# The h bias as SyncE's fourth transfer, transposed between dummy matmuls, in a linear-attention and squared-ReLU block

## The chip, the cores and the metric

The kernel runs on one core of a Trainium2 chip. The metric is device time in microseconds (us), the median of several runs. TensorE (PE) does the matmuls and transposes, VectorE (DVE) and ScalarE (ACT) the elementwise work and the evictions from PSUM, GpSimd (POOL) builds constants, and SyncE (SP) issues most DMA transfers.

## The reference

x has 2048 tokens of 448 features in bf16; there are 16 heads of 28. With xn the layer norm of x:

```python
qkv = xn @ wqkv                          # q, k, v by heads
pq, pk = phi(q), phi(k)                  # phi(t) = where(t > 0, t + 1, exp(t)) + 1e-6
kv  = einsum("bhsd,bhse->bhde", pk, v);  z = sum over s of pk
o   = (pq @ kv) / (pq @ z + 1e-6)
s   = o.reshape(...) @ wo
h   = relu(xn @ w1 + b1) ** 2            # 448 -> 1792
g   = silu(h @ w2 + b2)                  # 1792 -> 448
out = x + s * g
```

b1, the h bias, has 1792 numbers. Here it is used as a column of 128 numbers for each of the 14 parts of h.

## The kernel before, in words

The 2048 tokens are 16 tiles of 128. h is 14 parts of 128 features. The 448 input features are three chunks of 128 and a rest of 64; the rests of two token tiles, or of two parts, are multiplied side by side on the two halves of TensorE's rows.

Every operation is recorded with what it reads and writes. TensorE's and SyncE's operations keep the order in which they are recorded; those of the other engines are placed by a planner in the kernel, from assumed durations, due times and (for the first DMA transfers) a written table `landing` of arrival times. The planner also gives PSUM banks to TensorE's results. Semaphore waits are derived from the resulting order. For the first tiles the orders of VectorE and ScalarE are written out as chains (`bn0 ag0 ...`, `rs1 eT0.0 ...`), in which the bias copy `b1f` is the last on ScalarE's chain.

The head of the program, where the change lies:

- SyncE issues x of tile 0, tile 1, tiles 2 and 3; the main k weights (`load_main` with `w_k`, three chunks); the main weights of h parts 0 and 1 and their two rests; b1 as 14 rows of 128 (`b1r`, 256 bytes a row); then the weights of h parts 2 to 5, x of tiles 4 and 5, the weights of parts 6 to 9, x of tiles 6 and 7, the weights of parts 10 to 13, and the later loads. All go through the helper at L429. ScalarE issues the two k-weight rests itself.
- TensorE starts with dummy matmuls (`warm`, L1223), whose results nobody reads. `pe_transpose` (L604) transposes the three chunks of a normalized tile, `pe_transpose_rests` (L628) the rests of two tiles. `k_part` (L803) and `k_rests` (L818) make k of tiles 0 and 1, `head_part(lo, fi)` (L831) makes h part `fi` for tiles `lo` and `lo + 1` from the three main chunks, and `head_rest` (L847) adds the rests of parts 0 and 1 for all four tiles.
- `bias_cols` (L1238, L1241) transposes `b1r` on TensorE, a matmul of 14 rows by 14 columns, and ScalarE copies the result to `b1f`. ScalarE's and VectorE's bias-and-ReLU evictions of h (L766, L763) read `b1f`.
- Evictions of transposed tiles are at L613 and L614 (chunks) and L637 (rests).

After `head_rest` come, on TensorE, the other h parts of the first four tiles (L788), then k, q, the gate (L1094), sums over tokens and the attention product, in a written order. VectorE's transposes serve the later tiles.

The TensorE order of the head in the kernel before, by its own calls:

```python
        pe_transpose(0, ((0, 3, "act"),))
        warm(5)
        pe_transpose(1, ((0, 3, "act"),))
        ...
        head_part(0, 0)
        head_part(0, 1)
        pe_transpose_rests(2, "dve")
        head_part(2, 0)
        head_part(2, 1)
        bias_cols()
        head_rest(0)
```

Of the kernel before, what the change touches and what calls it, by code (L numbers as in the profile page):

```python
# [9 lines left out]
P = 128  # L10
S, D, F = 2048, 448, 1792
# [35 lines left out]
class Program:  # L47
# [6 lines left out]
    def add(self, eng, emit, reads=(), writes=(), dur=0.2, alts=(), nbytes=0, mode=None, label="", slow=1.0):  # L54
        op = Op(eng, emit, reads, writes, dur, alts, nbytes, mode, label)
        op.slow, op.behind, op.at = slow, None, None
        for t in op.reads:
            op.raw.add(self.writer[t])
            self.readers.setdefault(t, []).append(op)
        for t in op.writes:  # L60
            w = self.writer.get(t)
            if w is not None and w is not op:
                op.deps.add(w)
            for r in self.readers.get(t, ()):
                if r is not op:
                    op.deps.add(r)
            self.writer[t] = op
            self.readers[t] = [r for r in self.readers.get(t, ()) if r is op]
        op.raw.discard(op)
        op.deps |= op.raw  # L70
        for d in op.deps:
            d.succ.append(op)
        self.ops.append(op)
        return op
# [233 lines left out]
def bass_recurrent_scan__linear_attn_block__dense_activation_squared_relu__prompt_kernel(  # L308
    nc, A_x, A_wqkv, A_wo, B_x, B_w1, B_b1, B_w2, B_b2, out
):  # L310
    with ExitStack() as es:
# [24 lines left out]
        b1r = sb("b1r", [NF, P], bf)  # L336
# [83 lines left out]
        def tiles(t, lo, hi):  # L420
            if hi <= 2:
                return t[0][P * lo : P * hi].rearrange("(p s) d -> p s d", s=1)
            base, n = (2, 2) if hi <= 4 else (lo // 4 * 4, 4)
            v = t[0][P * base : P * (base + n)].rearrange("(p s) d -> p s d", s=n)
            return v[:, lo - base : hi - base, :]

        def dma(eng, dst, src, writes, nbytes, reads=(), dur=0.45, slow=1.0):
            return add(
                eng, lambda e, _: e.dma_start(dst, src), reads, writes, dur, nbytes=nbytes, label="dma" + str(writes[0]), slow=slow  # L429
            )  # L430

        def load_x(lo, hi, eng="sp"):
            dma(eng, x_tok[:, lo:hi, :], tiles(A_x, lo, hi), [("x", i) for i in range(lo, hi)], (hi - lo) * P * D * 2)

        def load_main(eng, w, src, name, lo, hi, c0=0, c1=3, off=0):
            dma(
                eng, w[:, c0:c1, lo:hi],
                src[128 * c0 : 128 * c1, off + lo : off + hi].rearrange("(c p) j -> p c j", p=P),
                [(name, c) for c in range(c0, c1)], 128 * (c1 - c0) * (hi - lo) * 2,
            )  # L440

        def load_rest(eng, w, src, name, lo, hi, off=0, part=None):
            for i in (0, 1) if part is None else (part,):
                dma(
                    eng, w[64 * i : 64 * i + 64, 3, lo:hi], src[384:448, off + lo : off + hi], [(name, 3 + i)],
                    64 * (hi - lo) * 2, ["actw"] if eng == "act" else (), dur=0.58,
                )
# [5 lines left out]
        load_x(0, 1, "sp")  # L453
        load_x(1, 2, "sp")
        load_x(2, 4, "sp")
        load_main("sp", w_k, A_wqkv, "wk", 0, D, off=D)
        load_rest("act", w_k, A_wqkv, "wk", 0, D, off=D, part=0)
        load_rest("act", w_k, A_wqkv, "wk", 0, D, off=D, part=1)
        load_main("sp", w_1, B_w1, "w10", cuts[0], cuts[1])
        load_rest("sp", w_1, B_w1, "w10", cuts[0], cuts[1], part=0)  # L460
        load_rest("sp", w_1, B_w1, "w10", cuts[0], cuts[1], part=1)
        dma("sp", b1r[:, :], B_b1.rearrange("(f p) -> f p", p=P), ["b1r"], F * 2)
        for i in (1, 2, 3):
            name = f"w1{i}"
            if i == 2:
# [130 lines left out]
        def pe_transpose(si, pieces):  # L596
            for lo, hi, eng in pieces:
                b = Buf("T")

                def f(e, _, lo=lo, hi=hi, b=b):  # L600
                    v = ps(b)[:, :].bitcast(bf)
                    last = None
                    for c in range(lo, hi):
                        last = e.transpose(v[:, (c - lo) * P : (c - lo + 1) * P], xn[:, si, c * P : (c + 1) * P], ident[:, :])  # L604
                    return last

                add("pe", f, [("xn", si), "ident"], [b], (0.107 if si < 2 else 0.0558) * (hi - lo), mode="128", label=f"T{si}.{lo}")

                def ev(e, eng, lo=lo, hi=hi, b=b):
                    src = ps(b)[:, 0 : 64 * (hi - lo)].bitcast(bf)  # L610
                    dst = xT[:, si, lo:hi, :].rearrange("p c k -> p (c k)")
                    if eng == "dve":
                        return e.tensor_copy(dst, src)  # L613
                    return e.activation(out=dst, in_=src, func=AF.Copy)  # L614

                n = hi - lo
                add(
                    eng, ev, [b], [("xT", si, c) for c in range(lo, hi)],
                    0.15 + 0.07 * n if eng == "dve" else 0.18 + 0.107 * n, label=f"eT{si}.{lo}",
                ).prio = -30  # L620

        def pe_transpose_rests(lo, eng):
            b = Buf("T")

            def f(e, _):
                v = ps(b)[:, :].bitcast(bf)
                for i in range(2):
                    last = e.transpose(v[:, i * P : (i + 1) * P], xn[:, lo + i, 384:512], ident[:, :])  # L628
                return last

            ts = (lo, lo + 1)
            add("pe", f, [("xd", i) for i in ts] + ["ident"], [b], 0.0558 * 2, mode="128", label=f"TR{lo}")

            def ev(e, eng):
                src = ps(b)[:, 0:P].bitcast(bf).rearrange("p (t k) -> p t k", t=2)
                if eng == "dve":
                    return e.tensor_copy(xT[:, lo : lo + 2, 3, :], src)  # L637
                return e.activation(out=xT[:, lo : lo + 2, 3, :], in_=src, func=AF.Copy)

            add(eng, ev, [b], [("xT", i) for i in ts], 0.39 if eng == "act" else 0.25, label=f"eTR{lo}").prio = -30  # L640
# [187 lines left out]
        def head_part(lo, fi):  # L828
            def f(e, _):
                for c in range(3):  # L830
                    last = e.matmul(  # L831
                        ps(head[fi])[:, lo * P : (lo + 2) * P], w_1[:, c, fi * P : (fi + 1) * P], xT[:, lo : lo + 2, c, :],
                        start=(lo == 0 and c == 0), stop=False, skip_group_check=True,
                    )
                return last

            add(
                "pe", f, [("w10", c) for c in range(3)] + [("xT", lo + i, c) for i in (0, 1) for c in range(3)] + ([head[fi]] if lo else []),
                [head[fi]], 3 * MM(256), mode="128", label=f"Ha{fi}.{lo}",
            )  # L840
# [376 lines left out]
        def warm(n, after=(), src=None):  # L1217
            b = Buf("W")

            def f(e, _):  # L1220
                last = None
                for _i in range(n):
                    last = e.matmul(ps(b)[:, 0:P], src or dum[:, 0:P], src or dum[:, 0:P], start=True, stop=True)  # L1223
                return last

            add("pe", f, ["dum", *after] if src is None else [], [b], n * 0.107, mode="128", label="warm")
# [8 lines left out]
        def bias_cols():  # L1235
            bb = Buf("B1")
            add(
                "pe", lambda e, _: e.transpose(ps(bb)[:, 0 : NF // 2].bitcast(bf), b1r[:, :], ident[0:NF, 0:NF]),  # L1238
                ["b1r", "ident"], [bb], 0.1, mode="128", label="B1",
            )  # L1240
            add("act", lambda e, _: e.activation(out=b1f[:, :], in_=ps(bb)[:, 0 : NF // 2].bitcast(bf), func=AF.Copy), [bb], ["b1f"], 0.2, label="b1f")  # L1241
# [2 lines left out]
        warm(30)  # L1244
        warm(4, [("mv", 0)])
        pe_transpose(0, ((0, 3, "act"),))
        warm(5)
        pe_transpose(1, ((0, 3, "act"),))
        warm(2)
        pe_transpose_rests(0, "dve")  # L1250
# [3 lines left out]
        k_rests(0)  # L1254
        pe_transpose(3, ((0, 3, "dve"),))
        head_part(0, 0)
        head_part(0, 1)
        pe_transpose_rests(2, "dve")
        head_part(2, 0)
        head_part(2, 1)  # L1260
        bias_cols()
        head_rest(0)

        byname = {op.label: op for op in pr.ops}
        for first, order in (
# [7 lines left out]
            if first < -26:  # L1273
                byname[names[0]].prio = first
        landing = {
# [3 lines left out]
        }  # L1279
        for (name, k), t in landing.items():  # L1280
# [136 lines left out]
```

## Time and profile before

| | |
|---|---|
| median of 3 runs | 143.07 us (143.07 to 143.12) |
| the profiled execution's own time | 142.37 us |
| its span, first to last instruction | 141.1 us |
| granted TensorE clock in the span | 1.00 |
| TensorE busy | 137.6 us, 1299 matmuls |
| VectorE, ScalarE, GpSimd busy | 104.0, 77.4, 6.3 us |
| DMA | 12.91 MB, mean 91 GB/s over the span |

Times in the profile are microseconds from the start of the span. A timeline line gives the start, the time from the first to the last of a group, the engine, the source line, the operation, the tiles and shapes, and in brackets the idle time before it with what ended it. PEld is TensorE's weight load, which runs beside its matmuls; the recorded end of a matmul includes the time to drain, so matmuls that follow each other overlap in the listing. SPq and ACTq are the issues of DMA transfers by those engines. A transfer has landed when the last of its completion marks is there; those times are read from the trace.

### The profile page before, as it was taken

What the parts mean: (1) busy time and instruction counts of PE and PEld (TensorE: products, weight loads), DVE (VectorE), ACT (ScalarE), POOL (GpSimd) and SP (SyncE); (2) the same over time, 40 slices, a digit from 0 to 9 for tenths busy, and PEclk for the clock granted to TensorE, in tenths of its full rate; (3) what the DMA queues carried; (4) which work ended last, traced back from release to release, by engine and by line L of the source; (5) the groups of instructions that cost most, each with busy time, mean ns of one, the idle gap of its engine ahead of it and who ended that gap; (6) DMA issues with size and microseconds to landing.
All of it is one profiled execution on the core that took longest, in us unless ns stands there. A gap on an engine that the chain in (4) does not pass through costs nothing.

```text
span 141.1 us, 3239 instructions
## 1 busy us (share of the span) xinstructions
PE 137.6 (97%) x1299; PEld 70.9 (50%) x1299; DVE 104.0 (74%) x226; ACT 77.4 (55%) x142; POOL 6.3 (4%) x40
## 2 busy tenths in 40 slices
PE   7999999999999999999999999999999999999992
PEld 7764445454444544444444444435447455555472
DVE  1988992999798898878867799695036516874875
ACT  3759993141988526986952867696138630301312
POOL 7900000000000000000000000000000000000000
PEclk9999999999999999999999999999999999999999
DMA  4999997249923000323000000000796001223033
GB/s 98 277 289 293 312 327 147 40 61 299 178 41 52 5 0 6 50 42 47 12 5 0 0 0 5 0 0 19 183 211 133 0 0 35 96 69 102 33 98 98
DMA packets 24220, 12.91 MB, mean 91 GB/s; under 512 B 14354, under 2 KB 23566, under 8 KB 24206
## 3 DMA queue, kind: packets, MB, share of 16 engines
q1 hardware_dynamic: 22414, 11.35, 31.9%
q10 hardware_dynamic: 1792, 1.36, 4.3%
q8 instruction: 10, 0.16, 0.5%
q14 instruction: 4, 0.03, 0.1%
HBM read 9.23 MB, written 1.90 MB: 79 GB/s over the span
## 4 chain that ended last, share of the span: by engine, by line
PE 93%; DVE 3%; DMA 1%; issue 0%
PE pb L788 29%; PE pb L1094 23%; PE pb L1186 8%; PE pb L889 7%; PE pb L731 7%; PE pb L741 6%; PE pb L1111 4%; PE pb L1151 3%; DMA x_tok<-in_A_x_dram 1%; PE pb L868 1%; DVE st L497 1%; DVE gbuf L1175 1%; PE pb L895 1%; PE pb L831 1%; PE pb L1038 1%; PE pb L803 1%
## 5 line engine op out<-in xcount | busy, mean ns | idle before, releaser
L788 PE MATMUL pb<-xT,w 64*128 64x512 bf16 x378 | 43.6, 376 | 0.0
L1094 PE MATMUL pb<-w,r 64*128 64x448 bf16 x336 | 34.6, 349 | 0.0
L766 ACT ACTIVATE r<-pb,b1f 128x512 bf16<-128x512 f32 x39 | 25.2, 686 | 12.3 <-PE pb L788 12.0
L788 PEld LDWEIGHTS pb<-xT,w 64*128 64x128 bf16 x378 | 18.4, 94 | 21.7 <-DMA w<-in_B_w_dram 0.2
L1094 PEld LDWEIGHTS pb<-w,r 64*128 64x128 bf16 x336 | 16.3, 94 | 15.9 <-issue 0.4
L778 ACT ACTIVATE r<-r 128x1024 bf16<-128x1024 bf16 x15 | 15.6, 1060 | 0.1
L763 DVE TENSOR_SCALAR r<-pb,b1f 128x512 bf16<-128x512 f32 x17 | 12.4, 745 | 4.1 <-PE pb L788 3.9
L1206 DVE TENSOR_TENSOR gbuf<-pb,gbuf 128x448 bf16<-128x448 f32 x14 | 8.1, 618 | 6.6 <-PE pb L1186 6.6
L497 DVE BATCH_NORM_STATS2 st<-x_tok 128x6 f32<-128x448 bf16 x16 | 9.4, 612 | 4.7 <-DMA x_tok<-in_A_x_dram 4.7
L731 PE MATMUL pb<-w_k,xT 64*128 64x448 bf16 x98 | 11.6, 349 | 0.0
L1134 ACT ACTIVATE gbuf<-gbuf 128x448 bf16<-128x448 bf16 x14 | 7.0, 570 | 7.5 <-DVE gbuf L1084 5.9
L741 PE MATMUL pb<-xT,w_q 64*128 64x512 bf16 x84 | 11.0, 376 | 0.0
L1186 PE MATMUL pb<-w_k,pqT 64*128 64x448 bf16 x96 | 10.6, 349 | 0.0
L1084 DVE TENSOR_TENSOR gbuf<-pb,b2b 128x448 bf16<-128x448 f32 x14 | 8.0, 614 | 3.4 <-PE pb L1094 2.0
L709 ACT ACTIVATE pk<-pb 128x448 bf16<-128x448 f32 x16 | 7.8, 543 | 3.7 <-PE pb L731 3.1
L721 DVE SCALAR_TENSOR_TENSOR pk<-pb,pk 128x448 bf16<-128x448 f32 x16 | 9.6, 619 | 0.2
L889 PE MATMUL pb<-pk,xn 128*128 128x448 bf16 x48 | 9.6, 353 | 0.0
L1002 DVE TENSOR_TENSOR pqT<-pqT,xT 128x2048 bf16<-128x2048 bf16 x3 | 3.7, 1223 | 7.8 <-DMA xT<-scr 7.8
L777 DVE TENSOR_TENSOR r<-r 128x1024 bf16<-128x1024 bf16 x13 | 8.5, 684 | 0.7 <-ACT r L766 0.6
L925 DVE TENSOR_TENSOR zacc<-zacc,pk 128x448 f32<-128x448 f32 x13 | 8.0, 618 | 0.1
L709 ACT ACTIVATE pqT<-pb 128x512 bf16<-128x512 f32 x12 | 6.5, 595 | 2.2 <-PE pb L741 2.2
L721 DVE SCALAR_TENSOR_TENSOR pqT<-pb,pqT 128x512 bf16<-128x512 f32 x12 | 7.7, 682 | 0.0
(100 smaller groups left out, 131.9 us busy)
## 6 DMA issues: line engine op xcount, KB each, us to landing
w<-in_B_w_dram SPq DMA_DIRECT2D x2, 784.0 KB, 7.9
out_dram<-gbuf SPq DMA_DIRECT2D x14, 112.0 KB, 1.7
w<-in_B_w_dram SPq DMA_DIRECT2D x3, 384.0 KB, 4.7
xT<-gbuf SPq DMA_DIRECT2D x32, 32.0 KB, 2.0
x_tok<-in_A_x_dram SPq DMA_DIRECT2D x2, 448.0 KB, 5.4
x_tok<-in_A_x_dram SPq DMA_DIRECT2D x3, 224.0 KB, 3.5
xT<-scr SPq DMA_DIRECT2D x6, 112.0 KB
xT<-scr ACTq DMA_DIRECT2D x5, 112.0 KB
```

What stands on the lines that cost most here:

```text
L497: add("dve", lambda e, _: e.bn_stats(st6[:, si, :], x_tok[:, si, :]), [("x", si)], [("st", si)], 0.61 if si > 3 else 0.6, label=f"bn{si}") ...
L709: "act", lambda e, _: e.activation(out=slot, in_=ps(buf)[0:rows, 0:n], func=AF.Exp), [buf, "actw"],
L721: lambda e, _: e.scalar_tensor_tensor(out=slot, in0=ps(buf)[0:rows, 0:n], scalar=1.0 + 1e-6, in1=slot, op0=ALU.add, op1=ALU.max),
L731: return e.matmul(ps(b)[:, 0:D], x_tile(rows, si, c), w_k[rows, c, :], start=start, stop=stop)
L741: return e.matmul(ps(b)[:, 0:512], w_q[rows, c, m * P : (m + 1) * P], x_group(rows, g, c), start=start, stop=stop,)
L763: return e.tensor_scalar(out=slot, in0=ps(b)[:, 0:512], scalar1=b1f[:, fi : fi + 1], scalar2=0.0, op0=ALU.add, op1=ALU.max)
L766: return e.activation(out=slot, in_=ps(b)[:, 0:512], func=AF.Relu, bias=b1f[:, fi : fi + 1])
L778: return e.activation(out=both, in_=both, func=AF.Square)
L788: return e.matmul(ps(b)[:, 0:512], w_1[rows, c, fi * P : (fi + 1) * P], x_group(rows, g, c), start=start, stop=stop,)
L889: last = e.matmul(ps(b)[:, 0:D], xn_cols(si, c * P, (c + 1) * P), pk[:, si, :], start=(si == 0), stop=(si == NT - 1),)
L1094: return e.matmul(ps(b)[:, 0:D], r_cols(rows, fi, si), w_2[rows, fi, :], start=start, stop=stop)
L1186: return e.matmul(ps(b)[:, 0:D], w, msb[rows, c, :], start=start, stop=stop)
```

## The change

b1 is fetched as SyncE's fourth transfer, right after x of tiles 2 and 3 and ahead of the main k weights, where before it was the eighth on this queue, behind the weights of h parts 0 and 1. Its transpose on TensorE stands between the transposes of tiles 0 and 1: two dummy matmuls, the bias transpose, two dummy matmuls, in place of five dummy matmuls. It no longer stands between the last `head_part` and `head_rest`. The rests of tiles 2 and 3 are transposed after h part 0 of tiles 0 and 1 instead of after part 1. The table of assumed arrivals has other numbers for the k weights, the weights of h parts 0 and 1, and b1; the table moves nothing by itself, but the planner's order and its choice of PSUM banks follow from it.

```diff
         load_x(2, 4, "sp")
+        dma("sp", b1r[:, :], B_b1.rearrange("(f p) -> f p", p=P), ["b1r"], F * 2)
         load_main("sp", w_k, A_wqkv, "wk", 0, D, off=D)
         load_rest("act", w_k, A_wqkv, "wk", 0, D, off=D, part=0)
         load_rest("act", w_k, A_wqkv, "wk", 0, D, off=D, part=1)
         load_main("sp", w_1, B_w1, "w10", cuts[0], cuts[1])
         load_rest("sp", w_1, B_w1, "w10", cuts[0], cuts[1], part=0)
         load_rest("sp", w_1, B_w1, "w10", cuts[0], cuts[1], part=1)
-        dma("sp", b1r[:, :], B_b1.rearrange("(f p) -> f p", p=P), ["b1r"], F * 2)
         for i in (1, 2, 3):
...
         pe_transpose(0, ((0, 3, "act"),))
-        warm(5)
+        warm(2)
+        bias_cols()
+        warm(2)
         pe_transpose(1, ((0, 3, "act"),))
...
         pe_transpose(3, ((0, 3, "dve"),))
         head_part(0, 0)
+        pe_transpose_rests(2, "dve")
         head_part(0, 1)
-        pe_transpose_rests(2, "dve")
         head_part(2, 0)
         head_part(2, 1)
-        bias_cols()
         head_rest(0)
...
         landing = {
-            ("x", 0): 2.8, ("x", 1): 3.45, ("x", 2): 4.45, ("wk", 0): 6.2, ("wk", 3): 6.1, ("wk", 4): 7.6, ("w10", 0): 7.25,
-            ("w10", 3): 7.55, ("w10", 4): 7.75, ("b1r", None): 7.95, ("w11", 0): 8.95, ...
+            ("x", 0): 2.8, ("x", 1): 3.45, ("x", 2): 4.45, ("wk", 0): 6.1, ("wk", 3): 6.1, ("wk", 4): 7.4, ("w10", 0): 7.1,
+            ("w10", 3): 7.45, ("w10", 4): 7.7, ("b1r", None): 4.6, ("w11", 0): 8.95, ...
```

In the built program the order of TensorE and SyncE differs in these places alone. On ScalarE the bias copy stands ahead of the exponentials of k tiles 0 and 1 instead of behind them. On VectorE the eviction of the rests of tiles 2 and 3 stands ahead of the two minima of k tiles 0 and 1 instead of between them, and for k tiles 2 and 3 the two minima stand ahead of the two maxima instead of in alternation.

2 rows, old and new, of the table landing are left out of this document.

## The prediction

> **What bounds the kernel now.** I read the page first, for which engine carries the span.
>
> ```profile
> PE 137.6 (97%) x1299; PEld 70.9 (50%) x1299; DVE 104.0 (74%) x226; ACT 77.4 (55%) x142; POOL 6.3 (4%) x40
> PE 93%; DVE 3%; DMA 1%; issue 0%
> ```
>
> TensorE is busy 97% of the span and carries 93% of the chain that ended last. A microsecond taken off TensorE's stream early is a microsecond at the end, provided that nothing which TensorE waits for holds it back later. So the question is local: what sets TensorE's times in the first 10 us, where the change lies. Next, TensorE's timeline there.
>
> ```profile
> 5.09 0.44 PE L1223 MATMUL pb<-dum 128*128 128x128 bf16 x5
> 5.74 0.34 PE L604 MATMUL pb<-ident,xn 128*128 128x128 bf16 x3 [0.20 <-DVE xn L527]
> 5.91 0.28 PE L1223 MATMUL pb<-dum 128*128 128x128 bf16 x2
> 6.03 0.28 PE L628 MATMUL pb<-ident,xn 128*128 128x128 bf16 x2
> 6.15 1.30 PE L803 MATMUL pb<-w_k,xT 128*128 128x448 bf16 x6
> ...
> 9.54 0.18 PE L1238 MATMUL pb<-ident,b1r 14*128 14x14 bf16 x1
> 9.65 0.39 PE L847 MATMUL pb<-xT,w 64*128 64x512 bf16 x2
> 9.87 0.59 PE L788 MATMUL pb<-xT,w 64*128 64x512 bf16 x4
> ```
>
> The first place: between the dummy matmuls (the last of the five starts at 5.32 in the trace) and the transpose of tile 1 at 5.74, TensorE waits for VectorE's normalized tile. That slot is free. The second: the bias transpose starts 0.11 us before the h rests at 9.65, and from there TensorE never pauses: the last h matmuls before it start at 9.33 and stream 0.11 us, so 0.10 us on each side of the bias transpose is a change of tile shape (128 rows, 14 rows, 64 rows). The same 0.10 us stands wherever the shape changes (7.39 to 7.54 between 128 and 64 rows, less 0.05 of streaming).
>
> Then SyncE's queue and the stretches of its DMA.
>
> ```profile
> 2.18 0.43 SPq L429 DMA_DIRECT2D w_k<-in_A_wqkv_dram  x1
> 2.66 1.74 SPq L429 DMA_DIRECT2D w<-in_B_w_dram  x3
> 4.45 0.61 SPq L429 DMA_DIRECT2D b1r<-in_B_b_dram  x1
> 5.10 1.56 SPq L429 DMA_DIRECT2D w<-in_B_w_dram  x3
> ```
>
> ```profile
> 5.00:6.00 1.00, 0.80 (x13) 0.63 (x11) 1.00 (x5) 0.77 (x3) 1.00 (x7) 1.00 1.12 312
> 6.00:7.00 1.00, 1.00 (x11) 0.59 (x9) 0.97 (x4) 0.93 (x4) 0.71 (x5) 1.00 0.85 178
> 7.00:8.00 1.00, 1.00 (x11) 0.45 (x10) 0.88 (x4) 0.29 (x3) 0.34 (x1) 1.00 0.98 322
> ```
>
> The last column is GB/s: 312, then 178 while the b1r packets (5.83 to 6.75) and the first packets of the next weights pass, then 322.
>
> Last, the landings, in the trace's marks. The k weights, issued at 2.18, land at 6.05; TensorE's first k weight load stands at 6.10, which is also where the loads before it would put it. Slack 0.00. The weights of h parts 2 to 5 land at 9.65, first load 9.69. The weights of h parts 10 to 13 land at 15.75 and hold a load, though no matmul:
>
> ```profile
> 15.79 0.23 PEld L788 LDWEIGHTS pb<-xT,w 64*128 64x128 bf16 x4 [0.20 <-DMA w<-in_B_w_dram]
> ```
>
> **The change part by part.**
>
> Removed: the bias transpose at 9.54. Without it the h rests follow the last h matmul (9.33 + 0.11 streaming + 0.10 change of shape) at 9.54, not 9.65: **-0.11 us**. The rests' other needs are there: their x tiles at 9.28 (eviction 8.99 to 9.28, earlier after the change), their weights at 7.58. The next load needs the landing at 9.65 and goes at 9.69; the matmul would now start at 9.76, 0.07 after that load, so the gain just passes. At 15.79 the load stands and the matmul follows at 15.92 in the trace; moved 0.11 earlier it would be at 15.81, still behind the load. So both covers hold with 0.02 to 0.07 us to spare, and not if those landings move later.
>
> Added: two dummies, the bias transpose, two dummies in place of five. Start 5.09, two dummies 0.11, change of shape 0.10, transpose about 0.01, change 0.10, two dummies 0.11: 5.52. The next transpose starts at 5.74 whatever happens, so cost 0, covered by VectorE's norm (5.25 to 5.68). Without that cover it costs 0.2. It also waits for b1r. That lands no sooner than the x transfer ahead of it (4.32), and by its own old time from issue to landing, 7.79 - 4.45 = 3.34, no later than 2.18 + 3.34 = 5.52. I take 4.5, since the small x transfer of 1.25 landed 2.0 us after issue in the emptier queue. Needed at 5.30, harmful beyond about 5.5: 0. If it is late, everything behind it on TensorE waits.
>
> The Trainium skill, "DMA: Bandwidth & Descriptors", section "Queues, rings and completion order", says that a completion mark lands only after every earlier write of the same DMA engine; by it b1r lands after 4.32 too, and no run here separates that from the queue's order.
>
> Moved on ScalarE: the bias copy (0.18) goes from 9.75 into the gap before the k exponentials (7.28 to 7.95): 0. At its old place ScalarE waited for the h rests until 10.14 anyway, so no gain. No queue but SyncE's has a DMA moved past it.
>
> Moved on TensorE and VectorE: the rests of tiles 2 and 3 transposed after h part 0 (8.35) instead of after part 1. Same instructions, no change of shape. Tile 3's eviction ends at 8.58 either way and sets the next h part at 8.73; the rests' eviction goes from 8.99 to about 8.70, ahead of the k minimum. VectorE sums the same to 10.0, then waits for x until 10.15. 0. The built order also has, at 25.7 to 27.5, two minima and then two maxima of k tiles 2 and 3 in place of alternating pairs: tile 2's bank comes free some 0.3 later, with TensorE in work that has its banks until 32.4. 0.
>
> Moved on SyncE: b1r goes ahead of the k weights and h parts 0 and 1, so these four are issued one transfer later, by 0.48 (the pitch 2.18 to 2.66) to 0.65 (b1r's own, 4.45 to 5.10); from the next weights on the issues stay or gain up to 0.17. What that costs is the one dear unknown. The k weights are issued at 2.66 to 2.83. The x transfer's first packet came 1.08 after issue (1.71 to 2.79), so theirs could go at 3.74 to 3.91. In the trace they went from 3.66 to 3.90, as each DMA engine finished its x packets, of which the last ran to 3.90. An engine loses 0 to 0.25, those that finish last (which set the landing) nearly nothing. Upper bound: the whole 0.65. Lower bound: 0, since an earlier landing would meet TensorE's own order at 6.10. I take **+0.05**, near the row of the last x packets. All six k matmuls, and with them the later head, shift by it. Weights of h parts 0 and 1, landed at 7.38 and 7.58, are needed at 7.96 and 9.54: 0 unless delayed by 0.6.
>
> The same page of the Trainium skill, "Specifications", gives about 0.6 us to the first byte on this path. By that the k weights would be ready at 3.26 to 3.43, wholly behind the x packets, and the term would be 0, the sum -0.11. The trace has 1.08 and decides.
>
> **Sum:** -0.11 + 0.05 = -0.06 us. The profiled execution took 142.37 (span 141.1 and 1.2 around it): 142.31. The median of the runs is 143.07, 0.70 above; carrying the same -0.06 over gives **143.01**.
>
> **The rivals.**
>
> Even: the k weights come 0.11 to 0.39 later, swallowing the gain. For it: zero slack at 6.10. Time 143.07 to 143.35.
>
> Slower: b1r's rows of 256 bytes carry the dip with them. From 6 to 7 us the stream moved 178 GB/s, against 312 before: (312 - 178) / 312 = 0.43 us lost. If that dip moves ahead of the k weights, they land at about 6.48, +0.43 - 0.11 = +0.32: 143.39, or with the whole issue delay of 0.65, 143.61. It decides once the k weights are over 0.11 late, and passes 0.2% at 0.39. Against it: the b1r packets took only 15 to 29 ns each, while first packets of the next weights took 180 to 530. The Trainium skill, same page, "Specifications", names 512 B as the least for full rate, with slower handling below; that speaks for this rival, the packets' own times against.
>
> Faster by more: the dip leaves the later stream. The weights of 9.65 and 15.75 land up to 0.43 earlier. In the profiled execution TensorE hardly waits for them, so this pays only if part of the 0.70 by which the runs exceed it is such waiting: -0.28 to -0.39, 142.68 to 142.79.
>
> That nothing moves (the bias transpose hidden at 9.54 after all) lies within the even case: 143.07.
>
> **How the numbers follow.** A measurement of this kernel tells about 0.2% (0.29 us) from no change. Forecast case, 142.96 to 143.07: 0.48. Even: 0.18. Both are within 0.2%: 0.66. Slower: 0.18. Faster by more: 0.16. The range takes the near ends of both outer cases, 142.75 to 143.45, and leaves out about half of each, some 0.17.
>
> **What would show it.** The bias transpose near 5.3 and the next transpose still near 5.74; b1r landed by 5.3; the first k matmul at 6.15 to 6.25; the h rests less than 3.50 after the first k matmul (3.39 by my sum); no idle at 15.8. Wrong, if the first k matmul starts after 6.5, if the transpose of tile 1 waits for b1r, or if TensorE pauses near 9.7 or 15.8.

## The result, and the profile after

The changed kernel takes 143.56 us (median of 22 runs, 142.99 to 145.28), the kernel before, in runs on the same chip, 143.12 us (22 runs, 142.58 to 143.66). The ratio is 1.0038, with a 95% interval of 1.0020 to 1.0056: slower by 0.44 us in medians, where 143.01 was forecast and the range ended at 143.45. The profiled execution of the changed kernel took 143.93 us with a span of 142.7; that of the kernel before, 142.37, is below all of its 22 runs here. Here and below, ratios and their intervals leave out single runs that stand far above the others of their kernel (one of the changed kernel's 22); the medians are of all runs.

The page of the changed kernel, its busy line and the shares of the chain that ended last:

```profile
PE 137.8 (97%) x1298; PEld 70.5 (49%) x1298; DVE 104.0 (73%) x226; ACT 77.2 (54%) x142; POOL 6.2 (4%) x40
PE 85%; DVE 6%; SPq 4%; DMA 3%; issue 0%
```

TensorE does the same work, 137.8 us against 137.6. But its share of the chain fell from 93% to 85%: the chain now runs through VectorE, SyncE's issues and DMA in the head. TensorE's timeline of the changed kernel says where (start, length of the group, engine, line, operation, tiles, shapes, number, idle time before it):

```profile
5.01 0.34 PE L604 MATMUL pb<-ident,xn 128*128 128x128 bf16 x3 [0.38 <-DVE xn L527]
5.19 0.28 PE L1223 MATMUL pb<-dum 128*128 128x128 bf16 x2
5.39 0.18 PE L1238 MATMUL pb<-ident,b1r 14*128 14x14 bf16 x1
5.50 0.28 PE L1223 MATMUL pb<-dum 128*128 128x128 bf16 x2
5.89 0.34 PE L604 MATMUL pb<-ident,xn 128*128 128x128 bf16 x3
...
6.79 1.31 PE L803 MATMUL pb<-w_k,xT 128*128 128x448 bf16 x6 [0.32 <-DMA w_k<-in_A_wqkv_dram]
...
10.19 0.39 PE L847 MATMUL pb<-xT,w 64*128 64x512 bf16 x2
10.41 6.37 PE L788 MATMUL pb<-xT,w 64*128 64x512 bf16 x56
17.46 3.20 PE L788 MATMUL pb<-xT,w 64*128 64x512 bf16 x28 [0.68 <-DVE mv L498]
20.50 0.92 PE L731 MATMUL pb<-w_k,xT 64*128 64x448 bf16 x8
21.25 0.92 PE L1094 MATMUL pb<-w,r 64*128 64x448 bf16 x8
```

The same view of the kernel before ends so:

```profile
18.94 0.92 PE L731 MATMUL pb<-w_k,xT 64*128 64x448 bf16 x8
19.69 0.54 PE L1094 MATMUL pb<-w,r 64*128 64x448 bf16 x4
```

Three steps make the whole difference. The first k matmul (L803) starts at 6.79 instead of 6.15, +0.64, and the line names the transfer of the k weights. The h rests (L847) start at 10.19 instead of 9.65: +0.54, for they come 3.40 us after the first k matmul, before 3.50. The gate's first matmuls (L1094) start at 21.25 instead of 19.69, +1.56; the further 1.02 us are pauses of TensorE among the h parts. From there on nothing differs: the own time less the start of L1094 is 143.93 - 21.25 = 122.68 after and 142.37 - 19.69 = 122.68 before. So the first 21 us set the end.

At 17.46 the view names VectorE's `mv`, which ended at 17.44; but these are the statistics of later tiles, which an h matmul doesn't read. The view of TensorE's weight loads names what held it, for the h parts 6 to 9 (13.58) and 10 to 13 (17.46):

```profile
13.58 2.70 PEld L788 LDWEIGHTS pb<-xT,w 64*128 64x128 bf16 x28 [0.48 <-DMA w<-in_B_w_dram]
17.46 1.62 PEld L788 LDWEIGHTS pb<-xT,w 64*128 64x128 bf16 x18 [1.18 <-DMA w<-in_B_w_dram]
```

SyncE's queue shows what was moved: the k weights are issued at 2.69 instead of 2.18.

```profile
2.19 0.46 SPq L429 DMA_DIRECT2D b1r<-in_B_b_dram  x1
2.69 0.40 SPq L429 DMA_DIRECT2D w_k<-in_A_wqkv_dram  x1
3.13 3.55 SPq L429 DMA_DIRECT2D w<-in_B_w_dram  x6
```

They land at 6.74 instead of 6.05: 0.51 later in the queue, 0.69 later in memory. In between the DMA stream moves less than half as much. Busy time by stretches of half a microsecond, where the last two columns are the DMA share and GB/s; first the kernel before:

```profile
4.00:4.50 0.50, 0.50 (x7) 0.50 (x6) 0.47 (x3) 0.32 (x2) 0.50 (x6) 1.00 0.98 269
4.50:5.00 0.50, 0.50 (x7) 0.33 (x5) 0.50 (x3) 0.42 (x2) 0.50 (x3) 1.00 1.05 350
```

and the changed kernel:

```profile
4.00:4.50 0.50, 0.50 (x9) 0.45 (x7) 0.47 (x2) 0.20 (x1) 0.50 (x6) 1.00 0.85 128
4.50:5.00 0.50, 0.13 (x3) 0.00 (x0) 0.50 (x3) 0.31 (x2) 0.50 (x4) 1.00 0.82 134
5.00:5.50 0.50, 0.49 (x6) 0.37 (x6) 0.50 (x2) 0.30 (x2) 0.50 (x5) 1.00 0.75 228
5.50:6.00 0.50, 0.40 (x5) 0.23 (x5) 0.50 (x3) 0.42 (x2) 0.50 (x4) 1.00 1.00 339
```

Before, the stream goes on at 269 to 350 GB/s after the x tiles. After, it moves 128 and 134 GB/s for a microsecond and needs until 5.5 to be full again. The DMA share of 0.85 hides a gap, for this view books a packet's whole time where it starts. Counted in the trace by starts and durations, 16 packets were under way at a time from 3.4 to 3.9 in both kernels, and from 4.0 to 4.4 17 before and 9 after. From 4.5 to 5.0 they are 14 again after the change, but some take long: of the k weights' 384, most of which take 41 ns, 23 of over 90 ns took 7.5 us together, one of them 1.03 us; before, 15 took 4.0 us. The packets' starts show it best. Before, the first of the k weights goes at 3.66, half of them have gone at 4.49, the last goes at 5.33. After, the first goes at 3.86, half at 5.51, the last at 6.27. The start is 0.20 late, the half 1.02. By 4.10 only 4 of the 384 have gone, before 74.

### The profile page after: what moved, and what is told of

It is laid out like the page before. It is cut to its first block, busy times and chain, and to the rows that moved or that the text cites. A ratio compares the mean times of both kernels' runs of the same rounds, so it can differ in the third digit from the quotient of the medians.

```text
span 142.7 us, 3238 instructions
## 1 busy us (share of the span) xinstructions
PE 137.8 (97%) x1298; PEld 70.5 (49%) x1298; DVE 104.0 (73%) x226; ACT 77.2 (54%) x142; POOL 6.2 (4%) x40
## 4 chain that ended last, share of the span: by engine, by line
PE 85%; DVE 6%; SPq 4%; DMA 3%; issue 0%
PE pb L788 24%; PE pb L1094 22%; PE pb L1186 7%; PE pb L889 7%; PE pb L731 6%; PE pb L741 6%; SPq L429 4%; PE pb L1111 4%; DMA x_tok<-in_A_x_dram 3%; PE pb L1151 3%; DVE st L497 2%; PE pb L868 1%; DVE gbuf L1175 1%; PE pb L895 1%; PE pb L1038 1%; DVE r L763 1%
## 5 line engine op out<-in xcount | busy, mean ns | idle before, releaser
L1094 PE MATMUL pb<-w,r 64*128 64x448 bf16 x336 | 34.6, 349 | 0.0
L1094 PEld LDWEIGHTS pb<-w,r 64*128 64x128 bf16 x336 | 16.3, 94 | 15.9 <-issue 0.4
```

What stands on the lines that cost most here:

```text
L1094: return e.matmul(ps(b)[:, 0:D], r_cols(rows, fi, si), w_2[rows, fi, :], start=start, stop=stop)
```

## The experiments

The question: what makes the k weights late? Theory one: their issue comes one transfer later, the x packets (the last ran to 4.01 in the kernel before) run out before enough k packets have followed, and that is all. Theory two, the prediction's slower rival: b1's short rows clog the stream, in b1's new seat (its place in SyncE's order). Theory three (A in the texts below): the k weights lose their place to the k rests, which ScalarE issues itself. Theory four: TensorE's new order. And beside it: why do the runs lose 0.44 when the profile shows 1.56?

One sum reads all runs. In every profile the own time is the first k matmul, plus the way to the h rests (3.4 to 3.5 in most), plus 10.04 to the gate when nothing is waited for, plus pauses for later weights, plus 122.7 (122.68 to 122.73 in all 17). Times in us; "pauses" is the gate's start less the h rests' less 10.04; the ratios are to runs of the kernel before on the same chip (medians 143.17 for the first four experiments, 142.93 for the next four, 142.99 for e9 to e12, 143.02 for the last three).

| kernel | k weights landed | first k matmul | h rests | pauses | median | ratio (95%) |
|---|---|---|---|---|---|---|
| before | 6.05 | 6.15 | 9.65 | 0.00 | 143.12 | 1 |
| after | 6.74 | 6.79 | 10.19 | 1.02 | 143.56 | 1.0038 (1.0020 to 1.0056) |
| e1_seat | 7.00 | 7.04 | 10.55 | 0.10 | 143.68 | 1.0040 (1.0023 to 1.0057) |
| e2_pe_noload | 6.45 | 6.49 | 9.89 | 0.67 | 143.36 | 1.0006 (0.9984 to 1.0028) |
| e3_noload | 6.01 | 6.36 | 10.04 | 0.10 | 143.02 | 0.9986 (0.9967 to 1.0005) |
| e4_pool | 6.28 | 6.80 | 10.19 | 0.13 | 143.01 | 0.9982 (0.9956 to 1.0009) |
| e5_rests_late | 7.75 | 8.04 | 12.24 | 0.01 | 145.05 | 1.0100 (1.0064 to 1.0137) |
| e6_long_rows | 7.17 | 7.21 | 10.72 | 0.01 | 143.86 | 1.0056 (1.0036 to 1.0075) |
| e7_pool_later | 6.65 | 6.70 | 10.10 | 0.43 | 142.73 | 0.9996 (0.9977 to 1.0015) |
| e8_pool_x6 | 5.80 | 6.10 | 9.48 | 0.69 | 142.70 | 0.9979 (0.9964 to 0.9994) |
| e9_wait | 7.62 | 7.67 | 11.18 | 0.01 | 143.82 | 1.0045 (1.0023 to 1.0068) |
| e10_wk_act | 6.16 | 6.34 | 9.76 | 1.01 | 143.52 | 1.0037 (1.0016 to 1.0058) |
| e11_x6_only | 5.95 | 6.34 | 9.88 | 0.49 | 142.96 | 0.9992 (0.9973 to 1.0012) |
| e12_pool_old_pe | 5.70 | 6.39 | 10.02 | 0.63 | 142.99 | 0.9997 (0.9977 to 1.0018) |
| e13_before_near | 5.99 | 6.63 | 10.13 | 0.01 | 142.76 | 0.9975 (0.9960 to 0.9990) |
| e14_after_near | 7.13 | 7.18 | 10.58 | 0.00 | 143.14 | 1.0004 (0.9985 to 1.0023) |
| e15_pool_near | 6.24 | 6.29 | 9.69 | 0.18 | 142.66 | 0.9974 (0.9959 to 0.9989) |

The first two columns tell when the k weights are what TensorE waits for. With the late issue the first k matmul follows the landing by 0.04 to 0.05 us in all kernels but e5_rests_late. With the early issue it does so, or nearly (0.04 to 0.18), in five of eleven; in the other six it comes 0.30 to 0.69 after the landing, behind the transposes and dummies that stand ahead of it on TensorE. In e13_before_near, for instance, x of tile 1 landed at 3.93 instead of 3.26, and the second tile's transposes start at 6.04 instead of 5.74. So part of a late landing is often covered.

**The seat alone.** The kernel before, with only the transfer moved:

```diff
         load_x(2, 4, "sp")
+        dma("sp", b1r[:, :], B_b1.rearrange("(f p) -> f p", p=P), ["b1r"], F * 2)
         load_main("sp", w_k, A_wqkv, "wk", 0, D, off=D)
...
-        dma("sp", b1r[:, :], B_b1.rearrange("(f p) -> f p", p=P), ["b1r"], F * 2)
```

> Only the transfer of b1r moves, to SyncE's fourth place; TensorE keeps the order of the kernel before (bias transpose at the end of the head, five dummies). Theory (the seat): the k weights, issued about 0.5 us later, land 0.5 to 0.7 later; the first k matmul stands at 6.6 to 6.85 and the h rests 3.50 after it, with no saving at the bias transpose, so 0.5 to 0.65 over the kernel before. Rival (a late engine in the later stream, by chance): first k matmul at 6.15, the k weights at 6.0 to 6.1, time within 0.2 of before. Rival (the new places on TensorE cost): as before, since TensorE's order is that of before.

TensorE's timeline of this run:

```profile
7.04 1.31 PE L803 MATMUL pb<-w_k,xT 128*128 128x448 bf16 x6 [0.62 <-DMA w_k<-in_A_wqkv_dram]
...
10.55 0.39 PE L847 MATMUL pb<-xT,w 64*128 64x512 bf16 x2
```

The whole loss is here, 1.0040 against the change's 1.0038, with TensorE's old order (3.51 from the first k matmul to the h rests). Theory four is out.

**TensorE's order without the transfer, and neither.** In the changed kernel, and in the one before, b1 isn't fetched; GpSimd fills `b1r` with zeros:

```diff
+        pool(lambda e, _: e.memset(b1r[:, :], 0.0), ["b1r"], dur=0.1).prio = -4
...
-        dma("sp", b1r[:, :], B_b1.rearrange("(f p) -> f p", p=P), ["b1r"], F * 2)
```

> The whole change on TensorE, but b1r is not fetched at all (it is filled with zeros by GpSimd, so the kernel leaves out the bias). Theory (the seat): with nothing ahead of the k weights the first k matmul is at 6.10 to 6.20, the h rests 3.39 after it, and the time is 0.1 to 0.3 under before. Rival (the new places on TensorE cost): the transpose of tile 1 or the first k matmul comes late all the same, 0.3 to 0.5 over before. Rival (chance in the later stream): somewhere from 0.1 under to 0.5 over, with waits at the h weights.

> The kernel before, with b1r not fetched (filled with zeros, so the bias is left out) and TensorE's order as before. It gives the price of the transfer in its old place: theory, 0 to 0.2 under before, as nothing that bounds the head waits for what comes behind it; first k matmul 6.15, h rests 3.50 after it; and 0.11 over the kernel with TensorE's change and no fetch. The rival by which small rows slow the stream wherever they stand: 0.3 to 0.4 under before.

Without the transfer in the fourth seat the k weights land at 6.45 and 6.01, and the loss is gone from both. The new order's 0.11 shows in the profile (3.40 against 3.68, of which 0.17 are a slower run of the k matmuls, 1.48 instead of 1.31), but not in the time: 1.0006 and 0.9986, overlapping.

**Another queue.** b1 is fetched by GpSimd, as its first instruction (`prio = -20`) or behind its first constants (`-4`):

```diff
+        dma("pool", b1r[:, :], B_b1.rearrange("(f p) -> f p", p=P), ["b1r"], F * 2).prio = -20
         load_x(2, 4, "sp")
-        dma("sp", b1r[:, :], B_b1.rearrange("(f p) -> f p", p=P), ["b1r"], F * 2)
```

> The change, with b1r fetched by GpSimd as its first instruction instead of by SyncE, so that SyncE has no transfer ahead of the k weights that was not there before, and one fewer behind them. Theory (the seat): b1r has landed by 4, first k matmul at 6.10 to 6.25, h rests 3.39 after it, 0.1 to 0.3 under before (142.8 to 143.0). Rival (small rows ahead of the k weights slow the stream, by whatever queue): first k matmul at 6.5 or later and 0.3 over before. Rival (the new places on TensorE cost): 0.3 to 0.5 over.

> The change, with b1r fetched by GpSimd behind its first constants (issue near 1.6 to 2.5) instead of as its first instruction, where it met the x transfer of tile 1 (landed 4.00 against 3.26). Theory (the seat on SyncE is the loss): x of tile 1 lands by 3.4, b1r by 5.0, first k matmul 6.10 to 6.30, h rests 3.39 after it; 142.7 to 143.0. If the later stream holds TensorE whatever the head does, 143.0 to 143.3 with idle before the h parts 10 to 13. If b1r ahead of the k weights costs by any queue: first k matmul at 6.5 or later, 143.4 or more.

As its first instruction, b1 lands at 4.17, but x of tile 1 comes at 4.00 (after: 3.76; before: 3.26), and the first transpose starts at 5.54. (That the fetch delays x isn't shown: x of tile 1 came at 3.93 in e13_before_near, without it.) Behind the constants, b1 lands at 5.03 and its transpose stands at 5.45. Both are back at the kernel before or slightly under it. The k weights land at 6.28 and 6.65: the landing scatters by some tenths even with nothing put ahead on SyncE. Half their packets had gone at 4.68 and 4.54, as in all kernels with the early issue (4.41 to 4.68).

**The rests held back.** In the changed kernel, ScalarE issues the k rests only when a constant of GpSimd's is there:

```diff
-                    64 * (hi - lo) * 2, ["actw"] if eng == "act" else (), dur=0.58,
+                    64 * (hi - lo) * 2, ["actw", ("hm7", 0)] if eng == "act" else (), dur=0.58,
...
+        byname["ln0"].behind = byname["dma('wk', 4)"]
```

GpSimd's constants are recorded earlier for this, and the last line places ScalarE's first statistics behind the rests.

> The change, with ScalarE's two k-weight rests held back by about 0.65 us (they wait for a GpSimd constant), so that they are issued behind the main k weights again, as in the kernel before, where the main k weights' packets went first. Theory A (lost place: behind b1r the main k weights also fall behind the first rest on ScalarE's queue, and the DMA engines share): the main k weights land at 6.1 to 6.4, the first k matmul is at 6.2 to 6.45 and half or more of the loss is gone: 143.1 to 143.4. Theory B (the issue delay of 0.50 alone): they land at 6.6 to 7.0 as in the change, time 143.5 to 143.8. In either case the transposes of tiles 0 and 1 may stand up to 0.2 later, as ScalarE's first statistics wait behind the rests' issues.

Now SyncE's k weights are issued at 2.70 and the first rest at 2.77, so they have their place again. They land at 7.75, later still. In the changed kernel 56 of the 128 packets of the rests had gone before 4.3; here none goes before 4.45, and half of the k weights' packets have gone only at 5.24. So the slow refilling needs no rests ahead, and theory three is not the cause; 56 packets of 41 ns on 16 engines would be 0.14 us. b1 is still ahead here. The run's time doesn't tell, though, for ScalarE's first statistics also start late (4.84, where the view names VectorE's `mv`), and with them TensorE's first transpose:

```profile
6.34 0.50 PE L604 MATMUL pb<-ident,xn 128*128 128x128 bf16 x3 [1.39 <-DVE xn L527]
```

which is 1.48 later than before. How much of the 1.0100 is that, and how much the k weights, stays open.

**Long rows in the seat.** The kernel without the fetch (e3_noload), with an unread transfer of 16 rows of 896 bytes as SyncE's fourth:

```diff
         load_x(2, 4, "sp")
+        dma("sp", spare[:, :], A_x[0][1024:1040], ["spare"], 16 * D * 2)
```

> TensorE's order of before, no fetch of b1r (zeros, the bias is left out), and in SyncE's fourth place a transfer that nobody reads: 16 rows of 896 bytes of x in place of 14 rows of 256 bytes. If the seat costs because any transfer delays the k weights: they land at 6.5 to 7.0, first k matmul 6.6 to 7.05, 143.4 to 143.8, like the kernel in which only b1r moved (143.68). If b1r's short rows or its 14 rows (fewer than the DMA engines) cost: they land at 6.0 to 6.3, 143.0 to 143.2, like the kernel with no fetch (143.02).

Its stretches of DMA:

```profile
4.00:4.50 0.50, 0.39 (x8) 0.22 (x4) 0.47 (x3) 0.27 (x3) 0.50 (x7) 1.00 0.84 176
4.50:5.00 0.50, 0.23 (x4) 0.23 (x5) 0.40 (x2) 0.46 (x2) 0.50 (x5) 1.00 0.90 219
5.00:5.50 0.50, 0.39 (x7) 0.21 (x4) 0.50 (x2) 0.35 (x1) 0.50 (x4) 1.00 0.81 200
```

The same dip, k weights at 7.17, 1.0056 (1.0036 to 1.0075), with no short row anywhere. Theory two falls: short rows aren't needed. Nor do short rows in that stretch suffice: with GpSimd's later fetch b1's 14 packets went at 3.64 to 4.19 in e8_pool_x6, e12_pool_old_pe and e15_pool_near, and the stream kept 327 to 373 GB/s from 4 to 5 us. The Trainium skill, "DMA: Bandwidth & Descriptors", section "Specifications", names 512 bytes as the least for full rate; here rows of 896 bytes cost no less than rows of 256 (1.0056 against 1.0040 in e1_seat).

**Lateness with nothing new ahead on SyncE.** Again the kernel without the fetch; SyncE's fourth transfer is the k weights, as before, but their issue waits for a constant of GpSimd's (the constants are recorded earlier again):

```diff
-        load_main("sp", w_k, A_wqkv, "wk", 0, D, off=D)
+        dma("sp", w_k[:, 0:3, 0:D], A_wqkv[0:384, D : 2 * D].rearrange("(c p) j -> p c j", p=P), [("wk", c) for c in range(3)], 384 * D * 2, [("hm7", 0)])
```

> TensorE's order of before, b1r not fetched (zeros, the bias is left out), no transfer in the fourth place; instead SyncE's issue of the main k weights waits for a GpSimd constant, so that it comes about 0.6 us later (2.7 to 2.9) with nothing put ahead of it. If the lateness of the issue alone is the loss (the DMA engines run out of work between the x transfer and the k weights): packets of the k weights from 4.0 to 4.2, a stretch from 4.0 to 4.5 at under 200 GB/s, landing at 6.7 to 7.2, first k matmul 6.75 to 7.25, 143.5 to 143.9 against 143.02 without the wait. If what was put ahead in the queue is the loss: landing at 6.1 to 6.4, 143.0 to 143.2.

Its queue, its stretches and TensorE:

```profile
2.90 0.39 SPq L430 DMA_DIRECT2D w_k<-in_A_wqkv_dram  x1
```

```profile
4.00:4.50 0.50, 0.50 (x7) 0.50 (x6) 0.47 (x3) 0.30 (x2) 0.50 (x7) 1.00 0.71 97
4.50:5.00 0.50, 0.50 (x7) 0.35 (x5) 0.50 (x2) 0.44 (x2) 0.50 (x5) 1.00 0.70 176
5.00:5.50 0.50, 0.50 (x7) 0.50 (x6) 0.50 (x2) 0.19 (x2) 0.50 (x4) 1.00 1.05 333
```

```profile
7.67 1.31 PE L803 MATMUL pb<-w_k,xT 128*128 128x448 bf16 x6 [1.06 <-DMA w_k<-in_A_wqkv_dram]
```

No new transfer lies ahead on the queue, the issue is 0.72 late, and the landing 1.57 late (7.62 against 6.05). The dip is there, and the loss, 1.0045 (1.0023 to 1.0068). The first packet goes at 3.96, 1.06 after the issue, half at 5.22. But ScalarE's rests do go ahead, as in the changed kernel: 63 of their 128 packets before 4.3. So the dip is there without the rests ahead (e5_rests_late), without b1 (e6_long_rows) and without any added transfer (e9_wait); what the late kernels share is the late issue. In all six whose SyncE issues the k weights a seat late or more (2.66 to 2.90), half their packets go at 5.10 to 5.68, and 6 to 11 packets are under way from 4.0 to 4.5 where the others have 16 to 17. That is theory one, as far as these runs go: none has the late issue with neither b1, nor the spare rows, nor the rests ahead, so that the lateness suffices by itself is argued from them together.

**The k weights on time, b1 still fourth.** In the changed kernel ScalarE issues the main k weights, and SyncE the two k rests behind b1:

```diff
-        load_main("sp", w_k, A_wqkv, "wk", 0, D, off=D)
-        load_rest("act", w_k, A_wqkv, "wk", 0, D, off=D, part=0)
-        load_rest("act", w_k, A_wqkv, "wk", 0, D, off=D, part=1)
+        dma("act", w_k[:, 0:3, 0:D], ..., ["actw"], dur=0.58)
+        load_rest("sp", w_k, A_wqkv, "wk", 0, D, off=D, part=0)
+        load_rest("sp", w_k, A_wqkv, "wk", 0, D, off=D, part=1)
```

> The change, with b1r still SyncE's fourth transfer, but the main k weights issued by ScalarE (near 2.1, its first transfer) and the two k-weight rests by SyncE behind b1r. If the issue time of the main k weights is what counts: they land at 5.9 to 6.4, first k matmul 6.1 to 6.45, h rests 3.39 to 3.5 after it, 142.7 to 143.0, though b1r is still ahead of the rest of SyncE's queue. If b1r's presence in that place slows the stream for whatever follows: they land at 6.6 or later, 143.4 or more.

ScalarE's issue at 2.11 has the k weights landed at 6.16, though b1 still goes fourth on SyncE. TensorE's timeline:

```profile
6.34 1.30 PE L803 MATMUL pb<-w_k,xT 128*128 128x448 bf16 x6
...
9.76 0.39 PE L847 MATMUL pb<-xT,w 64*128 64x512 bf16 x2
10.98 9.24 PE L788 MATMUL pb<-xT,w 64*128 64x512 bf16 x84 [0.83 <-DMA w<-in_B_w_dram]
```

The head is repaired, and the expected time was missed all the same. The weights of h parts 2 to 5, now issued at 5.76 instead of 4.91, land at 10.93 instead of 10.03, and TensorE loses at 10.98 what it won at 6.34. The dry stretch has moved to 6 to 7 us:

```profile
6.00:6.50 0.50, 0.50 (x8) 0.44 (x9) 0.50 (x2) 0.48 (x2) 0.44 (x3) 1.00 0.50 144
6.50:7.00 0.50, 0.50 (x5) 0.24 (x3) 0.47 (x3) 0.45 (x3) 0.29 (x1) 1.00 0.28 75
```

Here too a load behind the pushed seat had no room.

**What the later weights take.** First, x of tiles 6 and 7 issued behind the weights of parts 10 to 13, on e7_pool_later (e8_pool_x6) and on the kernel before (e11_x6_only); and b1 through GpSimd with the old TensorE order (e12_pool_old_pe):

```diff
-            if i == 2:
+            if i == 3:
                 load_x(6, 8, "sp")
```

> As the kernel with GpSimd's later fetch, and x of tiles 6 and 7 behind the weights of h parts 10 to 13 instead of ahead of them, so that those land 0.6 or more sooner. Theory that the later stream eats TensorE's gain: 0.2 to 0.5 under the kernel without this swap, no idle before h parts 10 to 13, 142.4 to 142.8. If it doesn't hold TensorE: the same time within 0.2. If VectorE needs x of tiles 6 and 7 earlier than I think: no faster, with waits at its statistics showing on TensorE.

> The kernel before with one thing changed: x of tiles 6 and 7 behind the weights of h parts 10 to 13. If those weights hold TensorE in ordinary runs: 0.1 to 0.3 under before (142.7 to 142.9). If the gain of the kernel with GpSimd's fetch and this swap came from the bias part: no change (142.9 to 143.1).

> b1r fetched by GpSimd behind its first constants, TensorE's order as before (the bias transpose at the end of the head). Against the kernel with the same fetch and the new order on TensorE (142.73) it gives what the new order is worth: 0.11 more (142.84) if the gap closed before the h rests reaches the end, the same if the later h weights hold TensorE anyway.

e8_pool_x6 has the lowest ratio of the full kernels: 0.9979 (0.9964 to 0.9994) to the one before. Its pause sits earlier, at the weights of parts 6 to 9, in its view of weight loads:

```profile
13.40 5.51 PEld L788 LDWEIGHTS pb<-xT,w 64*128 64x128 bf16 x54 [1.00 <-DMA w<-in_B_w_dram]
```

Neither half of it does that alone (0.9996, 0.9992), and by the intervals none of the three differs from the others for sure.

Then these waits were taken out: for the first four tiles the h parts 6 to 13 use the weights of parts 2 to 5, which have landed, on the kernel before, the changed one, and e7_pool_later:

```diff
-            names = wn("w1%d" % sum(fi * P >= c for c in cuts[1:]))
+            src = fi if g or fi < 6 else 2 + fi % 4
+            names = wn("w1%d" % sum(src * P >= c for c in cuts[1:]))
...
-                    ps(b)[:, 0:512], w_1[rows, c, fi * P : (fi + 1) * P], x_group(rows, g, c),
+                    ps(b)[:, 0:512], w_1[rows, c, src * P : (src + 1) * P], x_group(rows, g, c),
```

> The kernel before, but for the first four tiles h parts 6 to 13 are computed with the weights of parts 2 to 5, which are there earlier (so these parts are not the reference's); every transfer is still made. If the later weights hold TensorE in ordinary runs: 0.2 to 0.5 under before, with less spread, and no idle before those parts. If not: within 0.1 of before.

> The change with the same replacement of the weights of h parts 6 to 13 for the first four tiles. If the late k weights (about +0.65) and the saving (-0.11) both reach the end once no later wait stands behind them: 0.4 to 0.7 over the kernel before with the same replacement. If part of the change's loss comes from the later weights: under 0.3 over it.

> The new order on TensorE with GpSimd's later fetch of b1r and the same replacement. If the later weights took the saving: 0.1 to 0.2 under the kernel before with the same replacement, with the h rests 3.39 after the first k matmul and no idle before parts 6 to 13. If the saving is lost elsewhere: the same as that kernel.

The kernel before gains 0.26 us (143.02 to 142.76): that is what its ordinary runs wait for the later weights, though the profiled one waited for none. With the pauses gone from both, the changed kernel is 143.14 - 142.76 = 0.38 slower in medians. Their two profiles, first that of the kernel before and then that of the changed one, show the first k matmul so:

```profile
6.63 1.30 PE L804 MATMUL pb<-w_k,xT 128*128 128x448 bf16 x6
```

```profile
7.18 1.31 PE L804 MATMUL pb<-w_k,xT 128*128 128x448 bf16 x6 [0.55 <-DMA w_k<-in_A_wqkv_dram]
```

They differ by +0.55 there and -0.10 on the way to the h rests, 0.45 in all. The k weights landed 1.14 later (7.13 against 5.99), but only the second kernel waits for them. So the loss is the head's, and the profile's other 1.02 are pauses of which the runs of the kernel before have a share too.

## Why the prediction was wrong, point by point

- **The k weights one seat later, +0.05: this step failed.** It measured +0.64 at the first k matmul, and e9_wait, with a landing 1.57 late for an issue 0.72 late, broke the upper bound, by which a landing is delayed by no more than its issue. The start was estimated well: 3.74 to 3.91, and the first packet went at 3.86. The x packets, read as running to 3.90, ran to 4.01, which by the same argument would have covered more. But I priced the transfer by its first packet and let the rest follow at the old pace. Before, half of it had gone 0.83 after the first packet (3.66 to 4.49), straight behind the x packets; after the change, with the gap from 4.0 to 4.4, it took 1.65 (3.86 to 5.51). Of the issue's delay of 0.51, the x packets covered 0.31, as I had said; the other 0.20 were paid several times over. The Trainium skill ("DMA: Bandwidth & Descriptors", section "Specifications") gives about 0.6 us to the first byte on this path. The traces don't agree: from issue to first packet the k weights took 1.48 before, where x packets were still under way, and 1.06 in e9_wait, with the later issue.
- **The slower rival** had the place, the condition and nearly the price right (143.39 to 143.61; measured 143.56), but not the mechanism, so that its price fits is luck. Its short rows weren't needed (e6_long_rows), nor did an added transfer have to exist (e9_wait). Its chance of 0.18 was too low: zero slack at 6.10 was read, and should have counted for more, though that slack too was one execution's (0.30 to 0.69 in six of the kernels with the early issue).
- **The cover at 15.79, said to hold, did not.** (That at 9.69 held in the changed kernel: its weights landed at 10.03, and the h parts follow the rests by 0.22 as before; in e10_wk_act it broke.) The spare 0.02 to 0.07 us were those of one execution. The weights of parts 10 to 13 landed at 17.42 in the profile after (15.75 before), and at 16.76 in e2_pe_noload, which has no transfer in the seat. Those of parts 6 to 9, which the prediction didn't price, landed at 13.54 (12.42 before) and held TensorE too. e13_before_near puts 0.26 us on these waits in ordinary runs.
- **The bias transpose off the way to the h rests, -0.11: right in size.** 3.50 to 3.40 here, the same from e13_before_near to e14_after_near, and 3.51 in e1_seat against the changed kernel's 3.40 with the same fetch. That it reaches the end is not shown. Old and new order with the same fetch, or none: 1.0040 and 1.0038, 0.9986 and 1.0006, 0.9997 and 0.9996; intervals of 0.17 to 0.22% either way can't resolve 0.11 us.
- **The bias transpose among the dummies, 0: right.** b1 landed at 4.62 (predicted 4.5). The transpose stood at 5.39 and the next at 5.89, 0.15 later than before, as the first transpose was (5.01 against 4.86), with x of tile 1 landed at 3.76 instead of 3.26. The bias copy at 7.34 and the moved rests cost nothing that can be seen.
- **Faster by more** did not come: the later stream got no earlier. The weights of parts 2 to 5, issued 0.19 sooner (4.91), landed 0.38 later (10.03).

Open: why the stream refills so slowly when the issue comes late. The traces show few packets under way and then long ones, and give no cause.

## What to carry to other kernels

In a queue where the next transfer has no slack, a small transfer put ahead of it costs its issue, here 0.5 us, however few its bytes; and if the stream thins out meanwhile, the landing can be later still. A late transfer is priced by its whole course, by where half of it has gone and not by its first packet, and the delay of its issue is no upper bound for the delay of its landing. What is won early is kept only if the loads behind it have room: here a fetch through GpSimd's queue avoided the loss; with the later loads reordered as well the ratio was the lowest (0.9979), though a gain over the fetch alone isn't shown.

## What the runs showed of the hardware that was not expected

- Delaying the issue of one load of 336 KB by 0.5 to 0.7 us put its landing 0.7 to 1.6 us later than the 6.05 of the kernel before (after, e1_seat, e6_long_rows, e9_wait, e14_after_near). Single landings scatter (5.70 to 6.65 with the early issue, 6.74 to 7.75 with the late one); the stream from 4 to 5 us separates the two kinds clearly, with 57 to 219 GB/s in half a microsecond against 249 to 373.
- x of tile 1, issued at 1.25 to 1.27 in every kernel, landed anywhere from 3.19 to 4.00. Up to 3.39 the first transpose started at 4.74 to 4.86, from 3.76 on at 5.01 or later.
- A 3.5 KB fetch issued by GpSimd at 1.76 landed at 5.03, 3.27 us later, beside SyncE's queue in full work, and needed no place in it (e7_pool_later).
